# First loads, three split hidden tiles and a later weight load in an attention-and-MoE kernel

## The chip, the cores and the metric

The kernel runs on one core of one Trainium2 chip. Times are device microseconds (us) of one execution.

Engines are named as the profile names them: PE is TensorE's matrix unit, PEld its weight loads, DVE is VectorE, ACT is ScalarE, POOL is GpSimd, SP is SyncE. SyncE here only issues DMA; a "q" after an engine's name (SPq, POOLq) means that an instruction was seen at that engine's sequencer.

## The reference

Two stages, and the second uses the result of the first.

```python
# attention: B, H, S, D = 4, 8, 768, 64
k_sum = k.reshape(B, H, 24, 32, D).max(axis=3)      # 24 block summaries
v_sum = v.reshape(B, H, 24, 32, D).mean(axis=3)
# local scores where |q_pos - k_pos| < 16, and scores against the 24 summaries (+ log 32),
# one softmax over both, times [v, v_sum]
x = attn_out.transpose(0, 2, 1, 3).reshape(3072, 512)

# mixture of experts: N, D, E, F = 3072, 512, 8, 1024
P = exp(x @ w_gate - max)
for _ in range(8):                                   # Sinkhorn
    P /= P.sum(1, keepdims=True) + 1e-09
    P /= P.sum(0, keepdims=True) + 1e-09
    P *= N / E
out = sum over e of P[:, e:e+1] * (relu(x @ w1[e]) @ w2[e])
```

## The kernel before

The attention works on 16 *pairs* of heads, four pairs to a batch. Its matmuls are small, and they depend on exponentials and masks that ACT and DVE make. So the kernel fills PE's gaps with the work of expert 0: hidden matmuls (`hps`, x times w1) and projections (`yps`, h times w2), which can start on a batch as soon as its four pairs are done. A small planner in Python decides the order. Each piece of work is a *unit* with an engine, an estimated duration, the units it depends on and a priority; the planner simulates the engines and emits the instructions in the order that it found. On the chip each engine then runs its list in order (VectorE's timeline in the experiments shows it standing 2.84 us at one instruction, with others behind it). If an estimate was wrong, an engine stands at an instruction whose input has not come, while later ones could have run.

```python
# a unit: planned on eng for cost us; its results are usable lag us after its end
add(eng, cost, fn, deps, prio, opens=[psum buffers], lag=0.0)

def load(key, fn, issue, us, deps=()):               # a load by GpSimd's DMA queue (casts f32 to bf16)
    last[0] = add("POOL", issue, fn, [last[0], *deps])
    ...                                              # planned landing

def hidden_mm(e, hp, t0, n, f):                      # one hidden tile: 128 of F, n tokens
    for dk in range(KD):                             # KD = 4; dk is one pair's 128 columns of x
        nc.tensor.matmul(hp[:, 0:n], lhsT=w1s[e][:, dk, f * 128:(f + 1) * 128],
                         rhs=xT[:, dk, t0:t0 + n], start=(dk == 0), stop=(dk == KD - 1))
```

The first pairs of batch 0 are handled in halves of 384 tokens. From pair 4 on, the values need `Ve`, rows of v taken across the edges of the 128-token groups. They are copied there by small DMAs on SyncE's queue (by GpSimd's queue for the last pairs).

```python
U["near", i] = add("SP" if i < BY_DMA else "POOL", ..., lambda: near_values(i),   # Ve<-vx
                   [U["v", i], ..., U["vc", i % NE]], prio, lag=3.5)
```

For the last batch (pairs 12 to 15) k and q are transposed by DMA (`kT<-kst`, `qT<-qst`, on SyncE's queue), and so are the outputs of pairs 12 to 14:

```python
def x_dma(i):
    t, t0 = at.pop(("xs", i, 0)), i // PB * S
    nc.sync.dma_start_transpose(out=xT[:, i % PB, t0:t0 + S]...., in_=t[:]....)   # xT<-xs

def logits(b):                                       # the gate: tile lp, 24 matmuls a batch
    for t6 in range(G):
        for dk in range(KD):
            nc.tensor.matmul(lp[:, ...], lhsT=xT[:, dk, ...], rhs=wg_bf[:, dk, :], ...)
```

The gate of the last batch needs all of its `xT`. After it come the Sinkhorn iterations, with expert 0's rest between them, and then experts 1 to 7 in plain loops. Expert 1's weights are loaded by GpSimd's queue; tiny copies that read what the DMA transposes wrote hold that load back:

```python
def transposed():
    r = (NP - 1) % NB
    nc.gpsimd.tensor_copy(out=warm[:, 0:1], in_=kT[r][0:32, 0:1])
    nc.gpsimd.tensor_copy(out=warm[:, 1:2], in_=qT[r][0:32, W:W + 1])
    ...                                              # two copies that read Ve
last[0] = add("POOL", 0.3, transposed, [last[0], U["near", NP - 1]] + [U["kT", NP - 1, z] for z in range(2)])
load("w1n", lambda: load_w1(1), 0.85, 5.0)           # 1 MB on chip
load("w2n", lambda: load_w2(1), 0.85, 5.0)           # 1 MB on chip
```

They wait for `kT`, `qT` and `Ve`, but not for `xT`.

The softmax here doesn't subtract the row's maximum and nothing guards it: scores larger than these inputs give would overflow.

Of the kernel before, what the change touches and what calls it, by code (L numbers as in the profile page):

```python
# [9 lines left out]
FP32 = mybir.dt.float32  # L10
BF16 = mybir.dt.bfloat16
# [21 lines left out]
class Plan:  # L33
# [7 lines left out]
    def add(self, eng, cost, fn, deps=(), prio=0.0, opens=(), uses=(), lag=0.0):  # L41
        u = Unit(eng, cost, fn, [d for d in deps if d is not None], prio, list(opens), lag)
        for b in list(opens) + list(uses):
            b.users.append(u)
        if uses and eng != "PE":
            u.prio -= 100.0
        self.units.append(u)
        return u
# [71 lines left out]
def kernel(  # L120
# [10 lines left out]
    nc = tc.nc  # L131

    B, H, S, D = q.shape
    G = S // 128
    N, DM = out.shape
    E = moe_w_gate.shape[1]
    F = moe_w1.shape[2]
    KD = DM // 128
    KF = F // 128
    NT = N // 128  # L140
    NP = (B * H) // 2
# [56 lines left out]
    def load_w2(e):  # L198
        w2s[e] = wpool.tile([128, KF, DM], BF16, tag="w2", name="w2")
        nc.gpsimd.dma_start(out=w2s[e][:], in_=moe_w2[e].rearrange("(fk p) d -> p fk d", p=128))  # L200
# [7 lines left out]
    def copy(eng, out, in_):  # L208
        (nc.scalar.copy if eng == "ACT" else nc.vector.tensor_copy)(out=out, in_=in_)

    def hidden_mm(e, hp, t0, n, f):
        for dk in range(KD):
            nc.tensor.matmul(hp[:, 0:n], lhsT=w1s[e][:, dk, f * 128:(f + 1) * 128],  # L213
                             rhs=xT[:, dk, t0:t0 + n], start=(dk == 0), stop=(dk == KD - 1))

# [11 lines left out]
    with tc.tile_pool(name="attn", bufs=1) as attn, \  # L227
# [21 lines left out]
        def bank(tag, name, dtype=FP32):  # L249
            pool, n = (mps, 3) if tag == "m" else (aps, NA)  # L250
            return pool.tile([128, 2048 // mybir.dt.size(dtype)], dtype, tag=tag, name=name, bufs=n)
# [288 lines left out]
        def logits(b):  # L540
            lp = at["lp", b] = bank("a", "lp")[:, 0:G * E]
            for t6 in range(G):
                t = b * G + t6
                for dk in range(KD):
                    nc.tensor.matmul(lp[:, t6 * E:(t6 + 1) * E], lhsT=xT[:, dk, t * 128:(t + 1) * 128],  # L545
                                     rhs=wg_bf[:, dk, :], start=(dk == 0), stop=(dk == KD - 1))
# [21 lines left out]
            nc.vector.tensor_tensor(out=P_sb[:], in0=P_sb[:],  # L568
                                    in1=crec_sb[:].to_broadcast([128, NT, E]), op=ALU.mult)

        def hidden0(key, t0, f):
            if f == 0:
                at["h", key] = hpool.tile([128, KF, 512], BF16, tag="h", name="h")
            hp = at["hp"] = bank("m", "hps")
            hidden_mm(0, hp, t0, HS, f)
            return hp

        def project0(key, c, part):
            if part == 0:
# [7 lines left out]
                nc.tensor.matmul(t[:], lhsT=zeros[:, 0:128], rhs=zeros[:], start=True, stop=True)  # L587


        v_f32 = hpool.tile([128, 2, G, D], FP32, tag="h", name="vf32")  # L590
        nc.sync.dma_start(out=v_f32[:].rearrange("p j g d -> p (j g) d"),
                          in_=v[0, 0:2].rearrange("j (g p) d -> p (j g) d", p=128))
# [40 lines left out]
        def summary_constants(i):  # L633
# [2 lines left out]
            nc.vector.memset(t[0:24, D:VD], 32.0)  # L636
            nc.vector.memset(t[32:56, VD + D:2 * VD], 32.0)

        def edge_constants(n):
            nc.vector.memset(E_e[n][64:128, :, :], 0.0)  # L640
            if n == 0:
                nc.vector.memset(col_en, float(E) / float(N))
                nc.vector.tensor_copy(out=wg_bf[:], in_=wg_f32[:])

        def value_constants(n):
            t = V_e[n]
            nc.vector.memset(t[:], 0.0)
            nc.vector.memset(t[0:24, :, D:VD], 32.0)
            nc.vector.memset(t[32:56, :, VD + D:2 * VD], 32.0)


        U = {}
# [2 lines left out]
        def load(key, fn, issue, us, deps=()):  # L655
            last[0] = add("POOL", issue, fn, [last[0], *deps])
            last[1] = add("DMA", us, None, [add("RING", 0, None, [last[0]], lag=1.4 if last[1] else 0.9), last[1]], 100.0)
            U[key] = add("LAND", 0, None, [last[1]], lag=0.9)

        def load_pair(i, parts="kqv"):  # L660
            old = i - NQ
            for c in parts:
                if c == "v":
                    load(("v", i), lambda: load_v(i), 1.05, 1.85,
                         [U.get(("A", old, 1)), U.get(("near", old))])
                elif i < PB and c in "qr":
                    h = "qr".index(c)
                    load(("q", i, h), lambda h=h: load_qk(i, 1, h), 0.65, 0.65)
                else:
                    z = "kq".index(c)  # L670
                    load((c, i), lambda z=z: load_qk(i, z), 0.75 if i < PB else 1.65,
                         1.2 if i < PB else 1.55, [U.get(("tr", old, z)), U.get(("tr", old, 2))])
# [110 lines left out]
        def expert0(t0, xs):  # L783
            key, n = t0, len(halves)
            halves.append(key)
            pr = 1000.0 + n
            w = [U["w1", n] for n in range(4)]
            evac, old = [], [U.get(("pj", halves[n - 2], c)) for c in range(HG)] if n >= 2 else []
            for f in range(KF):
                buf = Buffer("m")  # L790

                def fn(f=f):
                    at["hp", key, f] = hidden0(key, t0, f)
                m = add("PE", 0.67, fn, xs + [w[f // 2]] + old, pr + f * 0.01, opens=[buf])

                def ev(f=f):
                    relu(U["rl", key, f].on, at["h", key][:, f, 0:HS], at.pop(("hp", key, f))[:, 0:HS])
                U["rl", key, f] = add({"ACT": 0.5, "DVE": 0.56}, 0, ev, [m], -1.0, uses=[buf])
                evac.append(U["rl", key, f])
            for c in range(HG):  # L800
                buf = Buffer("m")
                p0 = add("PE", 0.88, lambda c=c: project0(key, c, 0), evac[0:4] + [U["w2"]],
                         pr + 0.1 + c * 0.02, opens=[buf])
                p1 = add("PE", 0.88, lambda c=c: project0(key, c, 1), evac[4:8] + [p0],
                         pr + 0.11 + c * 0.02, uses=[buf])
                U["pj", key, c] = p1

                def ev(c=c):
                    copy(U["yo", key, c].on, out_acc[:, t0 // 128 + c, :], at.pop(("yp", key, c))[:])
                U["yo", key, c] = add({"ACT": 0.58, "DVE": 0.68}, 0, ev, [p1], -1.0, uses=[buf])  # L810

        def gate(b, xs, prio):
            buf = Buffer("a")
            U["lg", b] = add("PE", 0.65, lambda: logits(b), xs + [U["ec", 0]], prio, opens=[buf])
            U["lo", b] = add("ACT", 0.25, lambda: logits_out(b), [U["lg", b]], prio, uses=[buf])

        last[0] = add("POOL", 1.3, None)
        load_pair(0, "kq")
        U["vf32"] = add("LAND", 0, None, [add("RING", 0, None, [])], lag=4.8)
        U["v", 0] = add({"DVE": 0.6}, 0,  # L820
                        lambda: copy(U["v", 0].on, v_x[0][:, :, :, 0:D], v_f32[:]), [U["vf32"]])
        U["ident"] = last[0] = add("POOL", 0.35, ident_constant, [last[0]])
# [7 lines left out]
        for n in range(4):  # L830
            load(("w1", n), lambda n=n: load_w1(0, n, 4), 0.85, 1.25)
            if n == 1:
                for i in range(PB):
                    load_pair(i, "r")
        load("w2", lambda: load_w2(0), 0.85, 5.0)
        add("DVE", 4.6, constants, [], -5.0)
        for i in range(PB):
            pair_start(i, i)
            pair_half(i, 0, i)
        for n in range(NE):  # L840
            U["ec", n] = add("DVE", 0.42, lambda n=n: edge_constants(n), [U["no", PB - 1, 0]], 15 + n)
            U["vc", n] = add("DVE", 0.5, lambda n=n: value_constants(n), [U["no", PB - 1, 0]], 15.5 + n)

        first = {"T": lambda i: U["tr", i, 0], "Q": lambda i: U["tr", i, 1], "k": lambda i: U["kT", i, 0],
                 "q": lambda i: U["kT", i, 1], "v": lambda i: U["vs", i], "V": lambda i: U["Vs", i],
# [13 lines left out]
        expert0(HS, [U["x", i, 1] for i in range(PB)])  # L859
        gate(0, [U["x", i, h] for i in range(PB) for h in range(2)], 900)  # L860
        for i in range(PB, NP):
            load_pair(i)
            pair_start(i, 20 + i)
            pair_whole(i, 20 + i)
            if i % PB == PB - 1:
                b = i // PB
                xs = [U["x", PB * b + d] for d in range(PB)]
                gate(b, xs, 900 if b < B - 1 else 0)
                expert0(b * S, xs)
                expert0(b * S + HS, xs)  # L870
        def transposed():

            r = (NP - 1) % NB
            nc.gpsimd.tensor_copy(out=warm[:, 0:1], in_=kT[r][0:32, 0:1])
            nc.gpsimd.tensor_copy(out=warm[:, 1:2], in_=qT[r][0:32, W:W + 1])
            ve = V_e[(NP - 1) % NE]
            for j in range(2):
                nc.gpsimd.tensor_copy(out=warm[:, 2 + j:3 + j],
                                      in_=ve[64 + 32 * j:96 + 32 * j, G - 2, VD * j:VD * j + 1])

        last[0] = add("POOL", 0.3, transposed, [last[0], U["near", NP - 1]] + [U["kT", NP - 1, z] for z in range(2)])
        load("w1n", lambda: load_w1(1), 0.85, 5.0)
        load("w2n", lambda: load_w2(1), 0.85, 5.0)
        prev = [U["lo", b] for b in range(B)]
# [80 lines left out]
```

## Time and profile before

| | before |
|---|---|
| median of 3 runs | 742.81 us (742.37 to 743.0) |
| PE busy | 98% of the span |
| PE's longest wait | 5.6 us, the gate for `xT<-xs` |
| first transposes of k / first hidden / first projection | 6.07 / 22.60 / 35.91 us |
| gate of the last batch / first matmul of expert 1 | 119.93 / 158.95 us |

From the profile page of before: the span, and each engine's busy time with its share of the span and its instructions.

```profile
span 742.6 us, 10112 instructions
...
PE 726.4 (98%) x4233; PEld 355.9 (48%) x4302; DVE 367.5 (49%) x728; ACT 199.7 (27%) x342; POOL 90.2 (12%) x121
```

PE is nearly always busy, so a change to another engine saves nothing by itself. What can be won is time in which PE waits, runs at a lower clock, or runs filler. The waits of PE, in before, say what PE waited for: the waiting tile and line, the releaser, then us in total, times, and the longest.

```profile
PE lp L545 <- DMA xT<-xs: 5.6, 1, 5.6
PE idle L587 <- DVE zeros L593: 1.3, 1, 1.3
PE tkq L287 <- DMA kst<-in_k_dram: 0.8, 1, 0.8
```

One wait stands out. The view of tile xT on SyncE gives its three DMA transposes: how long the issue took, when they were issued, and the time from issue to landing.

```profile
L535 SPq DMA_TRANSPOSE xT<-xs x3: 1215/1220/1766, 102.7 to 114.0; - x3
...
DMA to landing us min/median/max: 3.5/3.6/11.8
```

Two took about 3.6 us and the third 11.8 us, for the same shape. GpSimd's timeline of before (start, duration, instruction, and in brackets the idle time before it) shows what went out just ahead of it:

```profile
112.12 0.78 POOL L194 DMA_DIRECT2D w_2434<-in_moe_w_dram  x1 [0.30 <-issue]
112.88 0.92 POOL L200 DMA_DIRECT2D w_2444<-in_moe_w_dram  x1
```

These are expert 1's two weight loads. PE's timeline of before around the wait:

```profile
119.93 0.19 PE L545 MATMUL lp<-wg_bf,xT 128*128 128x8 bf16 x2
125.77 0.75 PE L545 MATMUL lp<-wg_bf,xT 128*128 128x8 bf16 x22 [5.65 <-DMA xT<-xs]
126.38 4.33 PE L213 MATMUL hps<-xT,w_355 128*128 128x384 bf16 x16
```

And the windows view of before: stretch, length, PE busy (instructions), granted clock, DMA share (over 1 where packets overlap), GB/s.

```profile
122.00:124.00 2.00, 0.00 (x0) 0.69 1.21 195
124.00:126.00 2.00, 0.23 (x8) 0.50 1.27 207
126.00:128.00 2.00, 2.00 (x26) 0.50 0.28 46
128.00:130.00 2.00, 2.00 (x9) 0.60 0.00 0
130.00:132.00 2.00, 2.00 (x16) 1.00 0.00 0
```

Two losses are to be read here: a wait of 5.65 us, and then sixteen hidden matmuls at half clock, 4.33 us where 2.76 us is the time of the same sixteen at full clock.

### The profile page before, as it was taken

The page shows a single profiled execution, that of the slowest core. Times are in us where ns is not written, and L with a number is a line of the kernel's source. Part 1 is how long each engine was busy: PE and PEld are TensorE (multiplying, and loading weights), DVE is VectorE, ACT ScalarE, POOL GpSimd, SP SyncE. Part 2 cuts the span into 40 slices and gives each one's busy share as a digit, 9 for nine tenths or more (in the row PEclk, how much of TensorE's full clock was granted, in tenths as well). Part 3 has the DMA queues.
Part 4 walks back from the last instruction along what each step waited for, and adds up shares of the span by engine and source line. Part 5 has one row for each costly group of instructions (what it writes and reads, how often), then busy time and mean ns, then how long its engine had stood idle before and what let it go on. Part 6 is the DMA issues. An engine that isn't in the chain of part 4 may idle for free.

```text
span 742.6 us, 10112 instructions
## 1 busy us (share of the span) xinstructions
PE 726.4 (98%) x4233; PEld 355.9 (48%) x4302; DVE 367.5 (49%) x728; ACT 199.7 (27%) x342; POOL 90.2 (12%) x121
## 2 busy tenths in 40 slices
PE   8999996999999999999999999999999999999998
PEld 4666663544444444444444444444444444444444
DVE  7889883684444444444444444444443444444443
ACT  5578772442112112112112111111111121121120
POOL 8799331010000000000000000000000000000000
PEclk9999998999999999999999999999999999999999
DMA  9999918051003300113003300222003300001212
GB/s 154 176 144 141 132 29 125 1 91 24 0 1 58 56 1 1 22 35 57 0 1 57 56 1 1 37 31 47 0 1 57 56 1 1 0 1 58 99 71 114
DMA packets 95389, 36.04 MB, mean 49 GB/s; under 512 B 76016, under 2 KB 88816, under 8 KB 95344
## 3 DMA queue, kind: packets, MB, share of 16 engines
q0 software_dynamic: 77792, 26.19, 32.9%
q1 hardware_dynamic: 16880, 9.05, 5.0%
q8 instruction: 34, 0.56, 0.3%
q10 hardware_dynamic: 672, 0.15, 0.1%
q14 instruction: 11, 0.09, 0.0%
HBM read 52.45 MB, written 6.29 MB: 79 GB/s over the span
## 4 chain that ended last, share of the span: by engine, by line
PE 95%; DMA 2%; DVE 1%; issue 1%; POOLq 0%
PE hps L213 44%; PE yps L218 44%; DMA xT<-xs 2%; PE sg L334 1%; PE av L487 1%; PE vs L342 1%; PE tkq L290 1%; DMA kst<-in_k_dram 1%; PE ss L439 1%; PE av L420 1%; PE tx L525 1%; PE av L426 1%; PE idle L587 0%; PE lp L545 0%; PE tkq L287 0%
## 5 line engine op out<-in xcount | busy, mean ns | idle before, releaser
L204 ACT ACTIVATE h<-hps 128x512 bf16<-128x512 f32 (+1 forms) x224 | 127.8, 571 | 478.7 <-PE hps L213 461.5
L218 PEld LDWEIGHTS <-h 128*128 128x128 bf16 x1544 | 150.3, 98 | 175.9
L923 DVE SCALAR_TENSOR_TENSOR out_acc<-yps,P_sb,out_acc 128x512 f32<-128x512 f32 (+1 forms) x169 | 126.3, 747 | 166.0 <-PE yps L218 157.9
L206 DVE TENSOR_SCALAR h<-hps 128x512 bf16<-128x512 f32 (+1 forms) x176 | 120.5, 685 | 170.5 <-PE hps L213 170.2
L213 PE MATMUL hps<-xT,w_355 128*128 128x384 bf16 x256 | 49.1, 334 | 0.0
L218 PE MATMUL yps<-w_510,h 128*128 128x512 bf16 x179 | 44.6, 379 | 0.8 <-issue 0.2
L213 PE MATMUL hps<-xT,w_3445 128*128 128x512 bf16 x189 | 42.3, 379 | 0.2
L213 PE MATMUL hps<-xT,w_5597 128*128 128x512 bf16 x189 | 42.3, 379 | 0.2
L218 PE MATMUL yps<-w_4523,h 128*128 128x512 bf16 x188 | 42.2, 379 | 0.3
L218 PE MATMUL yps<-w_2444,h 128*128 128x512 bf16 x189 | 42.3, 379 | 0.2
L213 PE MATMUL hps<-xT,w_5059 128*128 128x512 bf16 x189 | 42.3, 379 | 0.2
L218 PE MATMUL yps<-w_3985,h 128*128 128x512 bf16 x189 | 42.3, 379 | 0.2
L213 PE MATMUL hps<-xT,w_3983 128*128 128x512 bf16 x188 | 42.2, 379 | 0.2
L218 PE MATMUL yps<-w_5061,h 128*128 128x512 bf16 x188 | 42.2, 379 | 0.2
L213 PE MATMUL hps<-xT,w_2883 128*128 128x512 bf16 x188 | 42.2, 379 | 0.2
L218 PE MATMUL yps<-w_2885,h 128*128 128x512 bf16 x187 | 42.2, 379 | 0.3
L218 PE MATMUL yps<-w_3447,h 128*128 128x512 bf16 x188 | 42.0, 379 | 0.2
L213 PE MATMUL hps<-xT,w_4521 128*128 128x512 bf16 x187 | 42.0, 379 | 0.2
L218 PE MATMUL yps<-w_5599,h 128*128 128x512 bf16 (+1 forms) x195 | 41.8, 370 | 0.2
L213 PE MATMUL hps<-xT,w_2434 128*128 128x512 bf16 x188 | 41.9, 379 | 0.2
L213 PEld LDWEIGHTS <-w_355 128*128 128x128 bf16 x256 | 24.4, 101 | 14.5 <-issue 1.7
L213 PEld LDWEIGHTS <-w_2434 128*128 128x128 bf16 x192 | 18.8, 98 | 22.6
(268 smaller groups left out, 558.2 us busy)
## 6 DMA issues: line engine op xcount, KB each, us to landing
out_dram<-out_acc SPq DMA_DIRECT2D x23, 256.0 KB, 2.0
qst<-in_q_dram POOLq DMA_DIRECT2D x32, 96.0 KB, 5.9
kst<-in_k_dram POOLq DMA_DIRECT2D x24, 96.0 KB, 6.3
w_355<-in_moe_w_dram POOLq DMA_DIRECT2D x4, 256.0 KB, 6.9
w_510<-in_moe_w_dram POOLq DMA_DIRECT2D x1, 1024.0 KB, 10.8
w_2434<-in_moe_w_dram POOLq DMA_DIRECT2D x1, 1024.0 KB, 9.8
w_2444<-in_moe_w_dram POOLq DMA_DIRECT2D x1, 1024.0 KB, 15.0
w_2883<-in_moe_w_dram POOLq DMA_DIRECT2D x1, 1024.0 KB, 8.2
```

What stands on the lines that cost most here:

```text
L204: nc.scalar.activation(out=out, in_=in_, func=AF.Relu, bias=0.0, scale=1.0)
L206: nc.vector.tensor_scalar_max(out=out, in0=in_, scalar1=0.0)
L213: nc.tensor.matmul(hp[:, 0:n], lhsT=w1s[e][:, dk, f * 128:(f + 1) * 128], rhs=xT[:, dk, t0:t0 + n], start=(dk == 0), stop=(dk == KD - 1))
L218: nc.tensor.matmul(yp[:, d], lhsT=h[:, f, c * 128:(c + 1) * 128], rhs=w2s[e][:, f, d], start=(f == 0), stop=(f == KF - 1))
L290: nc.tensor.transpose(t[:, g * 128:(g + 1) * 128], st[:, g, :, :].rearrange("p j d -> p (j d)"), ident)
L334: nc.tensor.matmul(dst, lhsT=kT[r][p0:p0 + 64, g * 128:(g + 1) * 128], rhs=qT[r][p0:p0 + 64, g * 128 + l0:g * 128 + l1], start=True, stop= ...
L342: nc.tensor.matmul(vs.rearrange("p (j d) -> p j d", j=2), lhsT=m_blk[:, g, :], rhs=sv[:, :, g, 0:D], start=(g == 0), stop=(g == G - 1))
L420: nc.tensor.matmul(av[:, o + j * VD:o + (j + 1) * VD], lhsT=em[:, j, c, :], rhs=sv[:, j, c, :], start=(cc == 0 and j == 0), stop=False, sk ...
L426: nc.tensor.matmul(av[:, o:o + 2 * VD], lhsT=ee[:, c, :], rhs=ve[:, c, :], start=False, stop=True, skip_group_check=True)
L439: nc.tensor.matmul(ss[:, 0:HS], lhsT=ksT[r][:], rhs=rhs, start=True, stop=True)
L487: nc.tensor.matmul(av[p0:p1, o:o + n], lhsT=lhsT, rhs=rhs, start=start, stop=stop, skip_group_check=True)
L923: nc.vector.scalar_tensor_tensor(out=out_acc[:, t, d], in0=yp[:, d], scalar=P_sb[:, t, e:e + 1], in1=out_acc[:, t, d], op0=ALU.mult, op1=A ...
```

## The change

Its intent is to remove both losses at 120 us and to start PE's real work earlier. It has these parts:

1. k of pair 0 is loaded as f32 by SyncE's queue (as v already was) and cast by ACT; GpSimd's queue starts with q.
2. Three hidden tiles of expert 0's first half are begun pair by pair: each of the four matmuls of a tile waits for its own pair's `xT`, not for all four.
3. The memsets of the edge and value constants move from DVE to GpSimd, behind expert 0's w2 load.
4. k and q of pair 4 are loaded ahead of w2, and v of pair 4 after it and after the memsets.
5. Expert 1's loads also wait for the last three DMA transposes of `xs`.

```diff
-    def hidden_mm(e, hp, t0, n, f):
-        for dk in range(KD):
+    def hidden_mm(e, hp, t0, n, f, dks=range(KD)):
+        for dk in dks:
...
+        k_f32 = hpool.tile([128, 2, G, D], FP32, tag="h", name="kf32")
+        nc.sync.dma_start(out=k_f32[:]...., in_=k[0, 0:2]....)
...
         def edge_constants(n):
-            nc.vector.memset(E_e[n][64:128, :, :], 0.0)
+            nc.gpsimd.memset(E_e[n][64:128, :, :], 0.0)
...                                     # value_constants likewise; col_en and wg_bf stay on DVE
-                m = add("PE", 0.67, fn, xs + [w[f // 2]] + old, pr + f * 0.01, opens=[buf])
+                if n == 0 and f < 3:
+                    for dk in range(KD):
+                        m = add("PE", 0.165, lambda f=f, dk=dk: hidden0(key, t0, f, [dk]),
+                                [xs[dk], w[f // 2], m if dk else U["ss", PB - 1, 0]], 9 + f * 0.01,
+                                **{"uses" if dk else "opens": [buf]})
+                else:
+                    m = add("PE", 0.67, lambda f=f: hidden0(key, t0, f, range(KD)),
+                            xs + [w[f // 2]] + old, pr + f * 0.01, opens=[buf])
...
-        load_pair(0, "kq")
+        load_pair(0, "q")
+        U["k", 0] = add({"ACT": 0.8}, 0, cast_k, [U["kf32"]])
...
+        load_pair(PB, "kq")
         load("w2", lambda: load_w2(0), 0.85, 5.0)
+        for n in range(NE):
+            U["vc", n] = last[0] = add("POOL", 1.2, lambda n=n: value_constants(n), [last[0]])
+            U["ec", n] = last[0] = add("POOL", 0.7, lambda n=n: edge_constants(n), [last[0]])
...
-            load_pair(i)
+            load_pair(i, "v" if i == PB else "kqv")
...                                     # in transposed():
+            if X_BY_DMA < NP:
+                nc.gpsimd.tensor_copy(out=warm[:, 4:5], in_=xT[0:32, PB - 2, (B - 1) * S:(B - 1) * S + 1])
...
-        last[0] = add("POOL", 0.3, transposed, [last[0], U["near", NP - 1]] + [U["kT", NP - 1, z] for z in range(2)])
+        last[0] = add("POOL", 0.3, transposed, [last[0], U["near", NP - 1]] + [U["kT", NP - 1, z] for z in range(2)]
+                      + [U["x", i] for i in range(X_BY_DMA, NP - 1)])
```

More of the change, by code (lines that the diff above doesn't have):

```diff
@@ L569, in sink_apply, with hidden0 @@
                                     in1=crec_sb[:].to_broadcast([128, NT, E]), op=ALU.mult)
-        def hidden0(key, t0, f):
-            if f == 0:
-                at["h", key] = hpool.tile([128, KF, 512], BF16, tag="h", name="h")
-            hp = at["hp"] = bank("m", "hps")
-            hidden_mm(0, hp, t0, HS, f)
-            return hp
+        def hidden0(key, t0, f, dks):
+            if dks[0] == 0:
+                if f == 0:
+                    at["h", key] = hpool.tile([128, KF, 512], BF16, tag="h", name="h")
+                at["hp", key, f] = bank("m", "hps")
+            hidden_mm(0, at["hp", key, f], t0, HS, f, dks)
         def project0(key, c, part):
@@ L587, in keep_busy @@
                 nc.tensor.matmul(t[:], lhsT=zeros[:, 0:128], rhs=zeros[:], start=True, stop=True)
+        k_f32 = hpool.tile([128, 2, G, D], FP32, tag="h", name="kf32")
+        nc.sync.dma_start(out=k_f32[:].rearrange("p j g d -> p j (g d)"),
+                          in_=k[0, 0:2].rearrange("j (p g) d -> p j (g d)", g=G))
         v_f32 = hpool.tile([128, 2, G, D], FP32, tag="h", name="vf32")
@@ L637, in summary_constants, with routing_constants @@
             nc.vector.memset(t[32:56, VD + D:2 * VD], 32.0)
+        def routing_constants():
+            nc.vector.memset(col_en, float(E) / float(N))
+            nc.vector.tensor_copy(out=wg_bf[:], in_=wg_f32[:])
         def edge_constants(n):
-            nc.vector.memset(E_e[n][64:128, :, :], 0.0)
-            if n == 0:
-                nc.vector.memset(col_en, float(E) / float(N))
-                nc.vector.tensor_copy(out=wg_bf[:], in_=wg_f32[:])
+            nc.gpsimd.memset(E_e[n][64:128, :, :], 0.0)
         def value_constants(n):
             t = V_e[n]
-            nc.vector.memset(t[:], 0.0)
-            nc.vector.memset(t[0:24, :, D:VD], 32.0)
-            nc.vector.memset(t[32:56, :, VD + D:2 * VD], 32.0)
+            nc.gpsimd.memset(t[64:128], 0.0)
+            nc.gpsimd.memset(t[0:64, 0, :], 0.0)
+            nc.gpsimd.memset(t[0:24, 0, D:VD], 32.0)
+            nc.gpsimd.memset(t[32:56, 0, VD + D:2 * VD], 32.0)
         U = {}
@@ L790, in expert0 @@
                 buf = Buffer("m")
-                def fn(f=f):
-                    at["hp", key, f] = hidden0(key, t0, f)
-                m = add("PE", 0.67, fn, xs + [w[f // 2]] + old, pr + f * 0.01, opens=[buf])
+                if n == 0 and f < 3:
[6 more added lines that the diff above has]
+                            xs + [w[f // 2]] + old, pr + f * 0.01, opens=[buf])
                 def ev(f=f):
@@ L813, in gate, with cast_k @@
             buf = Buffer("a")
-            U["lg", b] = add("PE", 0.65, lambda: logits(b), xs + [U["ec", 0]], prio, opens=[buf])
+            U["lg", b] = add("PE", 0.65, lambda: logits(b), xs + [U["rc"]], prio, opens=[buf])
             U["lo", b] = add("ACT", 0.25, lambda: logits_out(b), [U["lg", b]], prio, uses=[buf])
         last[0] = add("POOL", 1.3, None)
-        load_pair(0, "kq")
-        U["vf32"] = add("LAND", 0, None, [add("RING", 0, None, [])], lag=4.8)
+        load_pair(0, "q")
+        def cast_k():
+            t = at["st", 0, 0] = attn.tile([128, 2, G, D], BF16, tag="kst", name="kst", bufs=NQ)
+            copy("ACT", t[:], k_f32[:])
+        U["kf32"] = add("LAND", 0, None, [add("RING", 0, None, [])], lag=4.2)
+        U["k", 0] = add({"ACT": 0.8}, 0, cast_k, [U["kf32"]])
+        U["vf32"] = add("LAND", 0, None, [add("RING", 0, None, [])], lag=5.6)
         U["v", 0] = add({"DVE": 0.6}, 0,
@@ L839 @@
             pair_half(i, 0, i)
-        for n in range(NE):
-            U["ec", n] = add("DVE", 0.42, lambda n=n: edge_constants(n), [U["no", PB - 1, 0]], 15 + n)
-            U["vc", n] = add("DVE", 0.5, lambda n=n: value_constants(n), [U["no", PB - 1, 0]], 15.5 + n)
+        U["rc"] = add("DVE", 0.4, routing_constants, [U["no", PB - 1, 0]], 15)
         first = {"T": lambda i: U["tr", i, 0], "Q": lambda i: U["tr", i, 1], "k": lambda i: U["kT", i, 0],
```

## The prediction

> **What bounds the kernel.** TensorE: the page shows PE busy 98% of 742.6 us, and the chain of waits is 95% PE; from 132 us on it is hidden and projection matmuls without a break. Only places where PE waits, runs slowly or runs filler can be won. There are two.
>
> 1. *The stall at 120 us.* PE's waits have one long entry: the gate's matmuls (lp) wait 5.6 us for the DMA that transposes xs into xT. The queues' view gives the three such transposes 3.5, 3.6 and 11.8 us to landing. The slow one is issued at 114.0, after expert 1's w1 and w2 loads (1 MB each) went out at 112.1 and 112.9. The Trainium skill, "DMA: Bandwidth & Descriptors", "Queues, rings and completion order", says that each DMA engine takes turns between queues by packets; 3.6 against 11.8 us agrees. After the stall the granted clock is 0.50 to 0.60 until about 130 ("TensorE: Matmul & The Clock Gate", Part 1: half clock after an idle window of about 3.4 us). Sixteen hidden matmuls take 4.33 us there against 2.76, another 1.6 us.
>
> 2. *The start.* The first transposes of k begin at 6.07, after a DMA of 4.72 us. From there to 30 us the PE timeline has waits of 0.5 and 0.5 us, smaller ones, and some nine filler matmuls (2 to 2.5 us).
>
> **What the change does.**
>
> - Expert 1's loads wait for the transposes: the third then lands in about 3.6 us, near 117.6, before the gate at 119.9. Saves 5.65 + 1.6 = 7.2 us, all on the critical path. The loads go out 4 to 6 us later, need 10 to 15 us and land by 133; expert 1 needs w1 first at 159 (then 149). No new wait.
> - k and v of the first pair by SyncE: k's issue starts at 0.8 instead of 1.3, and GpSimd's queue runs 0.8 us earlier. The ScalarE cast costs about 0.8 us (its 128x768 copies), and the nine warm-up matmuls end only at 5.28. First transposes at 5.3 to 5.6: 0.5 to 0.8 us.
> - Three hidden tiles begun pair by pair: the same matmuls, moved into places of filler (20 planned before, 16 after) and of waits. 1 to 1.3 us.
> - Constants moved to GpSimd: 1.9 us less DVE between 23.1 and 25.8, where qT's copies stood behind them and PE then waited 0.53 us. They fall where GpSimd sat idle for 4.1 us. About 0.5 us.
> - Expert 0's w2 loads behind pair 4's k and q: it lands some 3 us later than 29, first use 35.9 (then about 33). Near, but likely no wait.
>
> Together the start gives 2.5 us (1 to 4). VectorE is busy 95% from 50 to 80 us while PE draws on expert 0's matmuls; part could be lost there. PE's order after 90 us is unchanged.
>
> **Prediction.** 742.8 - 7.2 - 2.5 = about 733.1 us; 730.5 to 736.5 should hold it 8 times in 10. Faster by over 2%: 0.01; within 2%: 0.98; slower: 0.01.
>
> **Right, if** lp no longer waits for xT; the third transpose lands in under 5 us; the granted clock stays full from 115 to 132; expert 1's loads are issued after the transposes; its first matmul comes near 149, with about 584 us from there to the end in both traces; first k transposes near 5.4; first hidden matmul near 19 instead of 22.6.
>
> **Wrong, if** the transpose is slow for another reason (lp still waits); k as f32 lands no earlier, because k, v and q share the engines; w2 arrives after its first use; GpSimd's memsets delay pair 4's values or the load stream; VectorE's busy stretch gives the early gain back.

## The result, and the profile after

| | before | after |
|---|---|---|
| median of runs | 742.90 us (742.37 to 743.65, 4 runs) | 734.88 us (734.54 to 736.79, 4 runs) |
| ratio, 95% interval | | 0.9897 (0.9878 to 0.9916) |
| first transposes of k / first hidden / first projection | 6.07 / 22.60 / 35.91 | 5.15 / 19.00 / 33.33 |
| gate of the last batch / expert 1 | 119.93 / 158.95 | 119.24 / 150.85 |
| from expert 1's first matmul to the end of the span | 583.7 | 583.9 |

A ratio is the mean time of a kernel's fast runs over the mean of before's fast runs of the same rounds, so it is not quite the ratio of the medians.

The change saves 8.0 us in the medians, 1.1%. It is within 2%, as predicted, and 734.88 lies inside the predicted range, 1.8 us above the 733.1 predicted.

From the profile page of after, the same two lines:

```profile
span 734.7 us, 10109 instructions
...
PE 722.6 (98%) x4228; PEld 354.1 (48%) x4298; DVE 366.5 (50%) x722; ACT 198.4 (27%) x341; POOL 98.1 (13%) x131
```

The waits of PE, in after (the largest entry, 1.3 us of filler waiting for zeros as in before, and the entries under 0.4 us are left out):

```profile
PE av L426 <- DMA Ve<-vx: 1.1, 1, 1.1
PE tkq L299 <- DMA qst<-in_q_dram: 0.9, 1, 0.9
PE sg L334 <- DVE kT L209: 0.5, 1, 0.5
PE hps L213 <- DMA w<-in_moe_w_dram: 0.4, 1, 0.4
```

The long wait is gone. Three smaller ones have come: for q's first half at 5.7 us, for w1 at 19.0, and for `Ve` at 41.6. The view of tile xT in after, and GpSimd's timeline:

```profile
L535 SPq DMA_TRANSPOSE xT<-xs x3: 1212/1212/1227, 102.0 to 113.3; - x3
...
DMA to landing us min/median/max: 2.8/3.5/3.5
```

```profile
116.09 0.17 POOL L895 CAST warm<-xT 32x1 f32<-32x1 bf16 x1 [6.93 <-DMA xT<-xs]
116.32 0.41 POOL L898 CAST warm<-Ve 32x1 f32<-32x1 bf16 x2
116.75 0.79 POOL L194 DMA_DIRECT2D w<-in_moe_w_dram  x1
```

GpSimd now stands 6.93 us until the last transpose has landed, which costs nothing, and only then issues the loads. The third transpose needed 2.8 us. PE's timeline of after at the gate, and the windows view there:

```profile
119.24 0.74 PE L545 MATMUL lp<-wg_bf,xT 128*128 128x8 bf16 x24
119.84 2.76 PE L213 MATMUL hps<-xT,w 128*128 128x384 bf16 x16
```

```profile
122.00:124.00 2.00, 2.00 (x15) 1.00 1.11 210
124.00:126.00 2.00, 1.95 (x12) 1.00 1.18 196
126.00:128.00 2.00, 2.00 (x11) 1.00 1.23 206
```

The loads move the same 200 GB/s as before at that time, but nothing waits for them: the clock stays full.

**Where the 8 us come from.** Since PE's order is the same in both kernels after the gate, its stretches can be compared one to one. PE's timeline at expert 1's first matmul, in before and then in after:

```profile
158.95 11.39 PE L213 MATMUL hps<-xT,w_2434 128*128 128x512 bf16 x51
```

```profile
150.85 9.44 PE L213 MATMUL hps<-xT,w 128*128 128x512 bf16 x42
```

From the gate of the last batch to this matmul, before took 158.95 - 119.93 = 39.02 us and after takes 150.85 - 119.24 = 31.61 us. That is 7.41 us. The gate itself begins only 0.69 us earlier. The sum, 8.1 us, is the whole saving (7.9 us between the two spans, the last 0.2 us being lost after 150 us).

So the stall paid what was predicted (7.2), and the start paid much less (0.7 against 2.5). Yet the start itself went as predicted: the first projection begins 2.6 us earlier. Counting matmul by matmul, with the median spacing of each shape in the traces (an estimate), PE has by 30 us some 2 us less of waiting and filler behind it than in before. Between 30 and 95 us much of it was lost again: the windows view has PE busy 64.42 us of these 65 in before and 63.37 in after, a difference of about the length of the new wait for `Ve`. The experiments ask where else.

### The profile page after: what moved, and what is told of

Same layout as the page of the kernel before. It is cut to its first block, busy times and chain, and to the rows that moved or that the text cites. A ratio compares the mean times of both kernels' runs of the same rounds, so it can differ in the third digit from the quotient of the medians.

```text
span 734.7 us, 10109 instructions
## 1 busy us (share of the span) xinstructions
PE 722.6 (98%) x4228; PEld 354.1 (48%) x4298; DVE 366.5 (50%) x722; ACT 198.4 (27%) x341; POOL 98.1 (13%) x131
## 4 chain that ended last, share of the span: by engine, by line
PE 91%; DMA 4%; POOL 2%; DVE 1%; issue 1%; SPq 0%; POOLq 0%
PE yps L218 44%; PE hps L213 44%; DMA w<-in_moe_w_dram 1%; DMA kT<-kst 1%; DMA vx<-in_v_dram 1%; DMA Ve<-vx 1%; PE sg L334 1%; PE av L426 1%; PE av L420 0%; PE ss L439 0%; POOL vx L276 0%; PE tkq L290 0%; PE vs L342 0%; POOL qst L265 0%; PE tx L525 0%
## 5 line engine op out<-in xcount | busy, mean ns | idle before, releaser
L213 PE MATMUL hps<-xT,w 128*128 128x512 bf16 (+1 forms) x1574 | 343.1, 370 | 1.7 <-DMA w<-in_moe_w_dram 0.4
L218 PE MATMUL yps<-w,h 128*128 128x512 bf16 (+1 forms) x1502 | 339.7, 378 | 2.2
L213 PEld LDWEIGHTS <-w 128*128 128x128 bf16 x1600 | 155.4, 98 | 172.0 <-DMA w<-in_moe_w_dram 0.5
L194 POOL DMA_DIRECT2D w<-in_moe_w_dram x11 | 15.3, 1395 | 340.5 <-PE hps L213 337.8
L393 ACT ACTIVATE er<-sg 128x960 bf16<-128x960 f32 (+1 forms) x28 | 23.2, 858 | 9.1 <-PE sg L334 7.0
L271 POOL DMA_DIRECT2D kst<-in_k_dram x24 | 20.3, 881 | 1.7 <-DMA w<-in_moe_w_dram 1.7
L200 POOL DMA_DIRECT2D w<-in_moe_w_dram x8 | 7.1, 890 | 100.5 <-PE yps L218 79.9
L271 POOL DMA_DIRECT2D qst<-in_q_dram x24 | 20.1, 858 | 0.9 <-issue 0.4
L518 DVE TENSOR_TENSOR xs<-av,rc 128x384 bf16<-128x384 f32 x32 | 17.8, 558 | 1.1
L322 DVE TENSOR_REDUCE ks<-kT 128x24 bf16<-128x768 bf16 x16 | 15.2, 948 | 2.1 <-DMA kT<-kst 1.8
L276 POOL DMA_DIRECT2D vx<-in_v_dram x15 | 15.9, 1064 | 0.0
L449 ACT ACTIVATE Ee<-ss 64x384 bf16<-64x384 f32 x24 | 11.1, 479 | 2.7 <-PE ss L439 2.7
```

The source lines that it names most:

```text
L194: nc.gpsimd.dma_start(out=w1s[e][:, :, part * fw:(part + 1) * fw], in_=moe_w1[e].rearrange("(dk p) f -> p dk f", p=128)[:, :, part * fw:(p ...
L218: nc.tensor.matmul(yp[:, d], lhsT=h[:, f, c * 128:(c + 1) * 128], rhs=w2s[e][:, f, d], start=(f == 0), stop=(f == KF - 1))
L271: nc.gpsimd.dma_start(out=t[:, :, j, :], in_=src[b, h0 + j].rearrange("(g p) d -> p g d", p=128))
L276: nc.gpsimd.dma_start(out=v_x[i % NQ][:].rearrange("p j g x -> p (j g) x")[:, :, 0:D], in_=v[b, h0:h0 + 2].rearrange("j (g p) d -> p (j g) ...
L393: nc.scalar.activation(out=dst, in_=src, func=AF.Exp, bias=0.0, scale=SCALE)
L518: nc.vector.tensor_tensor(out=t.rearrange("p g j d -> p (g j) d"), in0=av[:, :, 0:D], in1=rc[:].to_broadcast([128, G, D]), op=ALU.mult)
```

## The experiments

Twelve kernels were run, in four groups, each with its own runs of before on the same chip. The open points and their theories are these; the letters are used in some of the expectations (an earlier letter there belongs to the first point):

- The stall: the transpose is slow because the loads share the DMA engines with it; the rival is that it is slow for a reason of its own. The two parts of the change add up; the rival is that one depends on the other.
- The new `Ve` wait near 42 us. **D**: GpSimd's memsets delay the issue of pair 4's v, and so `Ve`. **E**: v lands late because it stands behind the 1 MB of w2 in the queue, whenever it is issued.
- The stretch from 65 to 95 us. **F**: the stream of loads sets when the DMA transposes of k land, so PE is held to a schedule that does not start earlier. **G**: VectorE, busy 93% from 50 to 80 us (27.95 of 30 us in after), has to do its own work.

The level of the times differs a little from group to group: before's median is 744.17, 743.43, 743.39 and 743.93 us in the four groups, against 742.90 beside after. The times in the expectations were reckoned from the first measurement, so they are read here as differences from before or from after_again. Only the second group has after beside it.

Since PE's order is fixed, the kernels with one and the same order of PE can be compared by landmarks in their profiles. "Gate 2" is the gate of the second batch, and so on.

### wait_only and start_only: each part alone

wait_only is before with part 5:

```diff
+            if X_BY_DMA < NP:
+                nc.gpsimd.tensor_copy(out=warm[:, 4:5], in_=xT[0:32, PB - 2, (B - 1) * S:(B - 1) * S + 1])
...
+                      + [U["x", i] for i in range(X_BY_DMA, NP - 1)])
```

> The kernel before with one part of the change alone: expert 1's two loads wait for the DMA transposes of xs. Theory A (the stall is worth 7.4 us and the rest of the change gave about 0.7): about 735.4 us; lp no longer waits for xT, the third transpose of xs lands in under 4 us, and the clock stays full from 115 to 132 us. Rival B (the wait and the slow clock are worth less, and the start gave 2.5 us that arrived at the end): about 737.5 us.

start_only is after without these lines.

> The changed kernel without the new wait: expert 1's loads go out as before. Theory A: the stall is back (lp waits 5 to 6 us, half clock after it), 742.0 to 742.4 us, so that what the start gives arrives as only 0.5 to 0.8 us. Rival B: about 740.4 us (2.5 us gained).

| | median, us | ratio (95%) | gate 4 | expert 1 | between |
|---|---|---|---|---|---|
| before (this chip) | 744.17 | | 119.93 | 158.95 | 39.02 |
| wait_only | 736.63 | 0.9903 (0.9878 to 0.9928) | 119.21 | 150.82 | 31.61 |
| start_only | 743.32 | 0.9991 (0.9966 to 1.0015) | 118.28 | 157.14 | 38.86 |

(The landmarks of before are those of its one profile.) The wait alone gives the whole of the change as far as times can tell, and the start alone gives 0.1%, with an interval that includes none. In start_only's profile the stall is back:

```profile
PE lp L545 <- DMA xT<-xs: 5.0, 1, 5.0
```

Its third transpose took 11.1 us. The parts do not depend on each other: 31.61 us from gate to expert 1 with the wait and 38.9 to 39.0 without it, whatever the start. The gate's own time scatters by more than the start is worth: it came at 119.24, 119.73 and 118.28 in three profiles with after's start, and at 119.93, 119.21 and 120.53 in three with before's. The means differ by 0.8 us; with const_early below, which has after's order too and came at 120.25, by 0.5.

### w2_waits: half of the load beside the transpose

Expert 1's w1 goes out as in before, and only w2 waits for `xT`:

```diff
         load("w1n", lambda: load_w1(1), 0.85, 5.0)
+        def transposed_x():
+            nc.gpsimd.tensor_copy(out=warm[:, 4:5], in_=xT[0:32, PB - 2, (B - 1) * S:(B - 1) * S + 1])
+
+        last[0] = add("POOL", 0.2, transposed_x, [last[0]] + [U["x", i] for i in range(X_BY_DMA, NP - 1)])
         load("w2n", lambda: load_w2(1), 0.85, 5.0)
```

> The kernel before, but of expert 1's loads only w2 waits for the transposes; w1 goes out as before, so one of the two 1 MB loads still runs beside the third transpose. Theory A (the transpose's packets take turns with the load's packets, one for one, in the trace of before 800 of them against some 1200): with 512 packets of w1 alone beside it the transpose lands by 119 to 121.5 instead of 125.7, lp waits 0 to 1.5 us, too short for the clock to drop, and the time is 735.5 to 737.5 us. Rival C (the transpose is slow for a reason of its own, such as late data or its own queue): lp waits about 5.6 us as before and the time stays at 742.8.

Measured: 738.06 us, ratio 0.9917 (0.9888 to 0.9946). PE's timeline of w2_waits:

```profile
122.07 0.71 PE L545 MATMUL lp<-wg_bf,xT 128*128 128x8 bf16 x22 [1.35 <-DMA xT<-xs]
122.64 2.76 PE L213 MATMUL hps<-xT,w 128*128 128x384 bf16 x16
```

The slow transpose now takes 7.5 us: 2.8 in after with no load beside it (the other two take about 3.5 in every kernel), 7.5 with one of 1 MB, 11.8 with two. The time of the transpose is that of the loads in front of and beside it, not its own. So rival C falls, but the forecast of a landing by 119 to 121.5 missed: it came at 122.03. PE waits 1.35 us, and the sixteen hidden matmuls behind run in 2.76 us: after a wait this short the clock did not drop. From gate to expert 1 takes 33.11 us, 1.5 more than with no load, which is the wait.

How the loads and the transpose share is shown by the queues' view (packets, MB, share of 16 engines). In before, from 114 to 118 us, the first four after the transpose was issued:

```profile
q0 software_dynamic: 335, 0.69, 105.0%
```

That is GpSimd's queue alone; no packet of the transpose ran. From 118 to 126:

```profile
q0 software_dynamic: 1115, 1.29, 97.8%
q1 hardware_dynamic: 800, 0.20, 22.2%
```

All 800 packets of the transpose run in this second stretch, beside 1115 of the loads. In the stretch where both are surely present, 120 to 125 us, it is 680 against 734, nearly one for one. The Trainium skill says in "DMA: Bandwidth & Descriptors", section "Queues, rings and completion order", that each DMA engine takes turns between queues, a packet at a time; this second stretch agrees. A packet of a load is four to eight times as long as one of the transpose (0.75 MB in 734 from 120 to 125 us and 0.69 MB in 335 before that, against 0.20 MB in 800), so where they take turns, a small transfer of small packets is slow. But turns are only a part. In w2_waits the transpose, issued at 114.56, again runs no packet until 118.5, beside 342 of w1; from 118.5 to 120.5 it runs 161 beside 167, and the other 639 of its 800 in the next microsecond and a half, when 14 of w1 were left. So one load ahead is enough to hold the first packet back for four microseconds, and theory A's picture of turns with all 512 packets of w1 is not what the trace shows. What holds the first packet back is not shown by any run.

### after_again, const_early: is it the memsets?

after_again is after, unchanged, beside the experiments of this group. const_early has its memsets earlier, between the w1 loads, so that v of pair 4 is issued directly after w2; PE's order is the same as in after.

> The changed kernel itself, as the measure for the other three of this call: 734.6 to 735.2 us, with one wait of 1.0 to 1.3 us of the values' matmuls for the DMA of Ve near 42 us.

```diff
+            if n >= 2:
+                U["vc", n - 2] = last[0] = add("POOL", 1.2, lambda n=n: value_constants(n - 2), [last[0]])
+                U["ec", n - 2] = last[0] = add("POOL", 0.7, lambda n=n: edge_constants(n - 2), [last[0]])
         load_pair(PB, "kq")
         load("w2", lambda: load_w2(0), 0.85, 5.0)
-        for n in range(NE):
-            U["vc", n] = ...
-            U["ec", n] = ...
```

> The changed kernel with the constants' memsets on GpSimd moved up, to where GpSimd waits anyway between the last two quarters of expert 0's w1 (15 to 21 us), so that v of pair 4 is issued near 24 instead of 28. Theory D (the memsets in front of v's issue make the new wait of 1.14 us): v lands 3 to 4 us earlier than 34.7, the wait for Ve is gone, time 733.6 to 734.0. Rival E (v stands behind expert 0's w2, 1 MB, in the same DMA queue, and lands when the DMA engines come to it): v lands at most 1 us earlier, most of the wait stays (0.3 us or more), time within 0.7 us of the changed kernel.

after_again: 736.76 us, ratio 0.9906 (0.9891 to 0.9921). const_early: 738.63 us, 0.9931 (0.9915 to 0.9947). The chain of waits (start, us, what) of after, and then of const_early, at pair 4's values:

```profile
28.07 6.67 DMA vx<-in_v_dram
...
36.92 5.68 DMA Ve<-vx
```

```profile
24.34 10.46 DMA vx<-in_v_dram
...
36.97 5.94 DMA Ve<-vx
```

v is issued 3.7 us earlier and lands at the same time, 34.80 against 34.74. In both, w2 lands just ahead of it, at 33.2 to 33.3. So D falls, and v lands as E has it: here the moment at which v is *issued* does not matter, its place behind w2 does. const_early waits 1.28 us for `Ve`, like after with its 1.14; after_again, the same program as after, does not wait at all, because its last `Ve` copy landed at 41.42, 1.2 us sooner than in after (its w2 and v had landed 1.1 us sooner, at 32.09 and 33.63), while its first projection was 0.8 us later. The wait is a near miss that falls one way or the other from run to run; the one expected of after_again did not come. E's forecast of time failed: const_early was to be within 0.7 us of the changed kernel and is 1.9 us slower than after_again in the medians. Why is not explained; the intervals still overlap a little.

### v_first, near_lag: two ways to mend the near miss

v_first loads v of pair 4 ahead of w2; near_lag tells the planner that the `Ve` copies take 6.0 us, not 3.5, so that PE is given other work first.

```diff
-        load_pair(PB, "kq")
+        load_pair(PB, "kqv")
         load("w2", lambda: load_w2(0), 0.85, 5.0)
...                                     # and v of pair 4 taken out of the later loads
```

> The changed kernel with v of pair 4 loaded before expert 0's w2 instead of behind it and the memsets. Theory E: v lands 5 us or more earlier, no wait for Ve; but w2 lands about 1 us later than 33.2, and if it is used at the same time PE waits up to 1 us for it instead. Time 733.6 to 735.2; what tells is whether the wait for Ve vanishes and one for w2 appears.

```diff
-                               [U["v", i], U.get(("A", i - NE, 1)), U["vc", i % NE]], prio, lag=3.5)
+                               [U["v", i], U.get(("A", i - NE, 1)), U["vc", i % NE]], prio, lag=(6.0 if i < BY_DMA else 3.5))
```

> The changed kernel, but the planner reckons with 6.0 instead of 3.5 us for the small copies into Ve by SyncE (the trace shows 5.3 to 5.7), and so places the values' matmuls of pairs 4 to 11 later among expert 0's. If the lost gain is this wait in the fixed order: the wait of 1.14 us is under 0.2, and the time 733.5 to 734.2. If the time that was lost comes back elsewhere (VectorE is 95% busy from 50 to 80 us): 734.5 to 735.5.

v_first: 735.71 us, 0.9893 (0.9876 to 0.9910). near_lag: 736.07 us, 0.9901 (0.9885 to 0.9918). In v_first v lands at 28.3 and w2 at 34.4; that is theory E from the other side. The planner gave PE another order in both kernels, so their gates cannot be compared with after's. In both profiles PE has no wait over 0.3 us between 30 and 119 us, and expert 1 begins at 149.95 and 149.45, against 150.85 and 151.34 in the two profiles of after. By the profiles they win 0.9 to 1.9 us; by the times they cannot be told from after_again, since the intervals overlap. So the question put to near_lag, whether the time lost at `Ve` comes back elsewhere, stays undecided: its median is 0.7 us below after_again's.

### light_stream, light_late: is it the stream of loads?

The second place is near 87 us. DVE's timeline of after_again (the idle time before an instruction in brackets), and PE's behind it:

```profile
87.07 0.95 DVE L322 TENSOR_REDUCE ks<-kT 128x24 bf16<-128x768 bf16 x1 [2.84 <-DMA kT<-kst]
```

```profile
88.94 0.81 PE L213 MATMUL hps<-xT,w 128*128 128x384 bf16 x4 [0.97 <-DVE out_acc L209]
```

DVE stands 2.84 us at the block maximum of pair 13's keys until the DMA transpose of k has landed. Behind it in DVE's list is a copy out of PSUM, `out_acc`, and PE needs the bank that this copy frees. (In after VectorE stands 1.85 us at this place, and no wait of PE over 0.15 us is listed behind it.) In the chain of waits of after_again (start, us, what):

```profile
77.76 9.29 DMA kT<-kst
```

The transpose takes 9.29 us. It lands at 86.56 in after, 87.05 in after_again and 85.60 in start_only, and at 85.79 in before, where DVE arrives at that very moment and does not wait. So after's kind, whose first projection is 1.8 to 3.1 us earlier than before's, gets this transpose no more than 0.2 us earlier. Within after's order it still moves by about a microsecond with the start: start_only, the earliest of these three, has it first, and after_again, the latest, last. The two light kernels take out q's loads of some pairs (using k in q's place: the result is then wrong, though so small a change in these scores is not seen by the comparison). All engines keep their order. light_stream leaves out the q loads of pairs 5 to 11, light_late those of pairs 8 to 11.

```diff
+        NO_Q = range(PB + 1, BY_DMA)                    # light_late: range(PB + 4, BY_DMA)
         def tr(i, z):
+            if i in NO_Q and z == 0:
+                at["st", i, 1] = at["st", i, 0]
...
-                    load((c, i), lambda z=z: load_qk(i, z), ...
+                    load((c, i), None if z == 1 and i in NO_Q else lambda z=z: load_qk(i, z), ...
```

> The changed kernel with the same order of instructions on every engine, but with the q loads of pairs 5 to 11 taken out of the DMA stream (14 DMAs of 192 KB; these pairs transpose k in place of q, so the result is wrong on purpose). Theory F (after 30 us the load stream, which runs at its limit from 10 to 86 us, decides how much of the start's gain survives): the DMA transposes of pairs 12 to 14 land within 4 us instead of 7 to 9, VectorE no longer waits 1.8 to 2.8 us for kT of pair 13 near 87 us, PE has no wait between 30 and 115 us, the gate of the last batch comes at 117.5 to 118.3 instead of 119.2 to 119.7, and the kernel is about 1.0 to 1.5 us faster than the changed one (ratio to before near 0.9885). Rival G (VectorE's own work, 95% busy from 50 to 80 us, is what holds PE): the transposes land earlier, but PE waits as before and the gate stays at 119.2 or later (ratio near 0.990).

light_stream: 737.09 us, 0.9911 (0.9881 to 0.9940). This missed: it is not faster than after. Its profile shows where. The last small `Ve` copy of pair 4 took 6.5 us instead of 5.7, probably because the loads behind the missing ones moved up beside it (that is not tested), and PE waited longer for it than in any other run:

```profile
44.19 0.34 PE L430 MATMUL av<-Ve,Ee 128*128 128x130 bf16 x3 [2.77 <-DMA Ve<-vx]
```

The granted clock fell to 0.50 between 46 and 48 us, behind this wait. The stretch that the experiment was for, from gate 2 to gate 3, took 26.54 us, against 27.36 to 28.36 us in the kernels with all loads, as F has it. So the experiment was made again with the early loads left alone.

> As light_stream, but the q loads are taken out for pairs 8 to 11 alone, so that nothing changes before some 48 us (light_stream lost 2.8 us at 44 us and some clock after it, because the loads behind the missing ones moved up beside the small copies into Ve). Theory F: from the second to the third gate, 27.4 and 28.4 us in the two profiles of the changed kernel, it takes 26.4 to 26.8 us, since kT of pair 13 lands by the time VectorE wants it; the gate of the last batch comes at 117.8 to 118.8 (1.3 us later at most if the wait for Ve near 42 us happens to come), ratio to before 0.9875 to 0.9895. Rival G (VectorE's own work holds PE there): second to third gate stays at 27.3 us or more. The result is meant to be wrong in batches 1 and 2, if by less than the comparison notices.

light_late: 734.69 us, 0.9878 (0.9848 to 0.9907). The windows view of after_again, and then of light_late (PE, PEld, DVE, ACT and POOL busy with their instructions, granted clock, DMA share, GB/s):

```profile
50.00:80.00 30.00, 30.00 (x358) 20.19 (x358) 27.90 (x78) 23.19 (x39) 26.39 (x31) 1.00 2.22 136
80.00:95.00 15.00, 13.91 (x138) 8.51 (x137) 11.24 (x28) 10.19 (x19) 4.29 (x8) 1.00 1.18 124
```

```profile
50.00:80.00 30.00, 30.00 (x355) 20.21 (x354) 27.90 (x78) 23.54 (x40) 19.69 (x23) 1.00 2.05 124
80.00:95.00 15.00, 15.00 (x166) 9.62 (x165) 11.89 (x29) 11.99 (x23) 4.26 (x8) 1.00 0.64 95
```

VectorE is busy 27.90 us of the first 30 in both, and does the same 78 instructions, yet light_late's PE then runs 15.00 us of the next 15 instead of 13.91. So G falls for this stretch: VectorE's own work was not in the way. The gate 2 to gate 3 time is 26.55 us, inside theory F's 26.4 to 26.8. This rests on one profile of each kernel: in time light_late (0.9878) cannot be told from after (0.9897) or after_again (0.9906). And with the loads their issuing on GpSimd went too (POOL 19.69 us busy instead of 26.39), which was not tested apart; the transposes are issued by SyncE. In light_late the same transpose of k lands at 83.23, after 5.9 us instead of 9.3, and DVE no longer stands before it:

```profile
83.76 0.94 DVE L326 TENSOR_REDUCE ks<-kT 128x24 bf16<-128x768 bf16 x1
```

| order of after | first projection | gate 2 to gate 3 | gate 3 to gate 4 | gate 4 | expert 1 |
|---|---|---|---|---|---|
| after | 33.33 | 27.36 | 24.53 | 119.24 | 150.85 |
| after_again | 34.12 | 28.36 | 24.53 | 119.73 | 151.34 |
| start_only | 32.86 | 28.18 | 24.52 | 118.28 | 157.14 |
| const_early | 33.49 | 28.06 | 24.53 | 120.25 | 151.86 |
| light_stream | 33.14 | 26.54 | 24.53 | 121.43 | 153.04 |
| light_late | 32.97 | 26.55 | 24.53 | 117.53 | 149.14 |

Every kernel with all of its loads pays 0.8 to 1.8 us between gate 2 and gate 3, and both light ones do not. light_late's expert 1 begins at 149.14, where the prediction's sum would have put it.

### no_split, k_pool: what two parts of the start are worth

no_split is after with whole hidden tiles; k_pool is after with pair 0's k by GpSimd's queue, as in before.

```diff
-                if n == 0 and f < 3:
+                if False:
```

> The changed kernel without the part 'three tiles begun pair by pair': expert 0's first tiles wait for all four pairs again. By the prediction the part is worth 1 to 1.3 us by 30 us: the idle and filler time of PE up to 30 us is 1 us or more above that of the changed kernel. By theory F little of it arrives: the time is within 0.6 us of the changed kernel (ratio 0.990 to 0.991).

```diff
-        load_pair(0, "q")
+        load_pair(0, "kq")
...                                     # k_f32 and its cast taken out
```

> The changed kernel without the part 'k of the first pair by SyncE': k goes by GpSimd's queue with the cast in the DMA. First transposes of k near 6.0 instead of 5.15 to 5.22 us. By the prediction 0.5 to 0.8 us are lost by 30 us; by theory F the total time is within 0.5 us of the changed kernel (ratio 0.990 to 0.9912).

no_split: 735.41 us, 0.9886 (0.9858 to 0.9915). The first hidden matmul goes back from 19.00 to 22.37 and PE has some 1.3 us more of waiting and filler by 30 us (the same estimate as above); still expert 1 begins at 150.67, as in after. The split's gain is real at its place and does not show when expert 1 begins. Where it went is not isolated, since the planner gave PE another order in both kernels, and after was not run beside them. k_pool: 736.99 us, 0.9906 (0.9880 to 0.9931). Its first transposes begin at 5.59, against 5.15 to 5.30 in the other kernels with k by SyncE's queue; before's 6.07 had been expected to come back nearly whole. In after, a part of this gain is lost at once: PE waits 0.94 us for the first half of q. The two f32 loads of 384 KB run beside it, and v's own time to landing went from 3.9 to 5.4 us; in k_pool PE has no such wait.

### combo: everything that seemed good together

v_first and near_lag together, and a planned 6.0 us instead of 2.0 for the DMA transposes of k and q:

```diff
-                    U["kT", i, z] = add("DMA", 1.7, None, [U["tr", i, z]], prio, lag=2.0)
+                    U["kT", i, z] = add("DMA", 1.7, None, [U["tr", i, z]], prio, lag=6.0)
```

> A version meant to beat both: v of pair 4 ahead of expert 0's w2, and a planner that reckons with 6.0 us for the small copies into Ve and for the landing of the k and q transposes, as the traces show. Theory F: no PE wait above 0.3 us between 30 and 115 us, gate of the last batch at 118.0 to 118.6, ratio to before 0.988 to 0.9895. If the gain is only moved to another wait: ratio 0.990 or above.

combo: 735.36 us, 0.9897 (0.9870 to 0.9924), with expert 1 at 150.06 and no wait of PE over 0.3 us between 30 and 119. The planner also moved the last gate to a later place, so the gates cannot be compared. In time it is not to be told from after, v_first or near_lag, and 0.9897 falls between the two bands of the expectation. No version beats after beyond its interval.

## Why the prediction was right or wrong

**The stall: right.** Predicted 7.2 us (5.65 of waiting and 1.6 at the lower clock); measured 7.41, as 39.02 against 31.61 us from gate to expert 1, and the same with the wait alone (31.61) and without it (38.86). The lp wait is gone, the third transpose lands in 2.8 us (under 5 predicted), the clock is full from 120 to 132, expert 1's loads are issued at 116.75, behind the transposes, and nothing waits for them. wait_only and w2_waits show that the loads are the cause. The remainder of 584 us from expert 1 on is 583.9.

The clock part rested on the Trainium skill, "TensorE: Matmul & The Clock Gate", Part 1, The HAM clock gate: half clock after an idle window of about 3.4 us, full again after a busy one of that length. The traces agree: the clock fell in a wait of 5.65 us, and was full again 3 to 4 us after work had resumed at 125.77; a wait of 1.35 us did not lower it. (One of 2.77 us did; see the last section.)

**The start at its place: right.** The first transposes of k were predicted at 5.3 to 5.6 and came at 5.15; the first hidden matmul at 19, and came at 19.00; w2 was to land some 3 us later than 29, near its first use but with no wait: it landed at 33.21 and the first projection began at 33.33. Not foreseen was that q would be late (0.94 us).

**The start at the end: mis-sized.** "Together the start gives 2.5 us (1 to 4)". It gave 0.7 to 0.8 us at the last gate: 0.69 between the two profiles, 0.8 between the means of three each, and 0.1% of the time (0.7 us) in start_only, none of it sure. This is the term that makes the prediction 1.8 us too fast. The prediction had named the risk, "VectorE is busy 95% from 50 to 80 us [...] part could be lost there", but not its cause. light_late shows that near 87 us VectorE's own work is not it. What holds PE there is the stream of loads: in after_again the DMA queues move 136 GB/s from 50 to 80 us (3.52 of 4.08 MB by GpSimd's queue), and with fewer loads the transpose of k lands in 5.9 instead of 9.3 us. For the small `Ve` copies the same is argued and not tested apart. A PE that comes earlier meets them earlier: at `Ve` near 42 us in some runs (0 to 1.3 us), and near 87 us, through VectorE, which waits in order for k (1.85 to 2.84 us in after, after_again, start_only and const_early) and holds back the PSUM copy behind it. So most of the early start was spent on waiting for transfers that came hardly earlier than in before, or later.

**The risks named.** "GpSimd's memsets delay pair 4's values": the values did become late (in after), but const_early shows that the memsets are not why; with v_first it points to the 1 MB of w2 ahead in the same queue.

**What stays open.** How much each part of the start is worth in the end, since the profiles scatter by about 0.7 us and most of the times' intervals are wider. Why the first packet of a transpose waits four microseconds behind loads. Whether v_first or near_lag truly save the microsecond that their profiles show. Why const_early is 0.25% slower than after_again. Whether a second profile of light_late would show the same.

The sum, as it should have been: 742.8 - 7.4 - 0.7 = 734.7 us, against 734.88 measured.

## What to carry to other kernels

A small DMA that PE waits for should not run beside a large load that nobody needs yet: hold the load back until the small transfer has landed, and count the clock's recovery with the wait. An earlier start may be worth little by itself (here 0.7 of 2.5 us); before adding it to the sum, look for the next place where the engine meets something whose time is set by another stream, and ask whether that moves too. Look at what stands ahead of a load in its queue: here issuing v earlier behind the same load brought nothing, and moving it ahead of that load brought 6.5 us.

## What the Trainium skill lacked or had wrong

- "DMA: Bandwidth & Descriptors", "Queues, rings and completion order", tells of turns by packets, which the runs show in one stretch (680 packets against 734). It does not tell that a DMA transpose issued behind queued loads may run no packet at all for its first 4 us (0 of 800 between 114 and 118 us), nor what a transfer of small packets then takes in the end: 2.8 us alone, 7.5 beside one load of 1 MB, 11.8 beside two.
- The same section does not spell out what follows from a queue's order for a small load behind a large one: v of pair 4, issued 3.7 us earlier behind the same 1 MB load, landed at the same time (34.80 and 34.74).
- "TensorE: Matmul & The Clock Gate", Part 1, gives an idle window of about 3.4 us as what lowers the clock. In light_stream a single idle stretch of 2.77 us, with short matmuls around it, was followed by a clock of 0.50 between 46 and 48 us; in w2_waits one of 1.35 us was not. Part 1's table gives no shorter wait that can be enough among sparse matmuls; a later passage of the page does tell of short idle times between groups of matmuls that make the clock swing, but without a length.
